# First expert's weights taken up later, an early partition maximum on GpSimd, and one more attention step ahead of the experts

## The chip, the cores and the metric

The kernel runs on 1 core of one Trainium2 chip. The metric is the device time of one execution in microseconds (us), and the time of a kernel is the median of several executions. The engines are named as in the profile: PE is TensorE, PEld its weight loads, DVE is VectorE, ACT is ScalarE, POOL is GpSimd, SP is SyncE, whose only work here is to issue DMAs.

## What is computed

Three layers follow each other. Attention in chunks of 64 tokens gives 4608 rows of 512; each row is sent to the best of 8 experts (two matrices with a ReLU between them, scaled by the gate); the result goes through an MLP with a piecewise quadratic activation.

```python
scores = scale * np.matmul(q_c, k_c.transpose(0, 1, 2, 4, 3))
attn = np.exp(scores - np.max(scores, axis=-1, keepdims=True))
attn = attn / (np.sum(attn, axis=-1, keepdims=True) + 1e-09)
x = np.matmul(attn, v_c)                      # then 4608 x 512
...
expert_idx = np.argmax(x @ w_gate, axis=1)    # 8 experts
for e in range(E):
    h = np.maximum(xe @ w1[e], 0.0)           # 512 -> 1024
    out[mask] = gate_w[mask, None] * (h @ w2[e])
...
h = x @ w_in                                  # 512 -> 2048
g = np.where(h >= 1, h, np.where(h <= -1, 0.0, (h + 1) ** 2 / 4))
return g @ w_out
```

## The kernel before

The order of the instructions on PE, ACT, DVE and SP is written out by the program itself (`manual_schedule`); each engine works through its own list from front to back, and an instruction that waits holds up all that stand behind it on its engine.

**Attention.** `attention_step(i)` works on one tile of 128 tokens, in stages of neighbouring tiles: the scores of tile i (L474), the transposed probabilities of tile i-1 (L482), the transposed result of tile i-3 (L502), the product with v of tile i-2 (L494), the gate logits of tile i-4 (L562) and the same by token for tile i-5 (L569). `vector_work(i)` adds what ACT does (copies `pt` L509, `xc` L513, the exponential `p` L522, `lt` L547) and what DVE does (row maximum `mx` L518, difference `p` L521, `rd` and `xr` L534 to L538). The 36 tiles are loaded in pairs: at each odd step SP issues q, k and v for a later pair, and it stores the finished pair `xr` to `xd` in DRAM (L541). The pool of `xr` has two buffers, so the buffer of one pair is written again three steps after its store was issued. Steps are numbered by the tile i in what follows.

**Gate.** The tiles are counted in batches of 6, 6, 6, 4, 6, 5 and 3. For each batch `gate(b)` works out on DVE the place of each token in the list of its expert (`m` to `slot`), with a few counting matmuls on PE in between (L594 to L598), and POOL scatters the tokens into `ld` in DRAM, one indirect DMA per tile (L635). After batch 0 the first expert is chosen; after batch 3 (`CUT_BATCH`) the rows of the first window of tokens are fetched: a list gather (L172), three row gathers `xg` (L149), a row maximum (`xam`, L102), the split into two half-precision parts (`xh`), and a DMA transpose into `xtw` (L168). After the last batch `rank_experts` orders the other experts and the second window is fetched in the same way.

**Experts' weights.** `fetch_experts` loads the eight pieces of the two matrices of an expert into seven buffers `raws` (L232, 512 KB each). `make_experts` turns them into two half-precision parts: four squares on ACT with a sum (L108, one per piece), the sum over pieces on DVE (`am_w`, L267), a maximum over the partitions on POOL (`partition_all_reduce`, L105, output `ag_w`), six small DVE operations that make a power of two of it (`kb` L79 to L90, `s_w`, `i_w` L91), then four times a high part on ACT (L111) and a low part on DVE (L114), which frees the buffer.

**What sets the order.** These background jobs are generators. A planner with four clocks (`clk`, in us of its own reckoning, PE's clock advanced by `slot`, 1.15 three times in an attention step) places each piece of background work when its engine's clock is not ahead of PE's by more than a slack, and not before the time that the job asks for. For a loaded piece of weights that time is the issue plus `WEIGHTS` (4.5). So a job's place in an engine's list is fixed when the program is built; on the chip its instruction waits if the data is late.

**Start of the experts.** The attention steps 0 to TAIL - 1 are written out ahead of the first window of the experts; from `HOLD` on, background jobs other than the urgent ones are held. `gate_tail` puts the remaining steps between the first matmuls of the first window, `ffn` L1000: each call of `beside` (after every three matmuls, or after the ReLU) advances it by one `yield`. The window is 384 tokens: 96 matmuls `h` (L1000), then 72 matmuls `y` (L1032). Then the second window of the same expert follows, then the other experts with their weights, and from about 620 us on the MLP (L1268, L1234).

Of the kernel before, what the change touches and what calls it, by code (L numbers as in the profile page):

```python
# [8 lines left out]
F32 = mybir.dt.float32  # L9
# [9 lines left out]
P = 128  # L19
NT = 36  # L20
# [18 lines left out]
AHEAD = 3  # L39
PACE = 3.5  # L40
LIST, ROWS, WEIGHTS = 2.2, 3.0, 4.5
LIST0, ROWS0 = 4.0, 9.0
SLACK = 0.3, 0.6
URGENT = 1.5
SIDE = 5, 7, 7
TAIL = NT + 2
HOLD = NT + 1
SIZES = {4: (4,), 5: (2, 3), 6: (3, 3), 7: (4, 3)}
ENOUGH = 11
# [7 lines left out]
def build(ctx, tc, qT, kT, v1, wg, w1, w2, wi, wo, out):  # L57
    nc = tc.nc
    pe, act, dve, pool, sp = nc.tensor, nc.scalar, nc.vector, nc.gpsimd, nc.sync
# [10 lines left out]
    with tc.manual_schedule(engines={E_.PE, E_.Activation, E_.DVE, E_.SP}):  # L70
# [33 lines left out]
        def allmax(dst, src):  # L104
            pool.partition_all_reduce(dst, src, channels=P, reduce_op=bass.bass_isa.ReduceOp.max)  # L105
# [11 lines left out]
        early = rows.enter_context(tc.tile_pool(name="early", bufs=1, side="right"))  # L117
# [10 lines left out]
        def raw_piece():  # L128
            nraw[0] += 1
            return raws_[:, (nraw[0] - 1) % NRAW]  # L130
# [98 lines left out]
        def load_weights(m, a, row):  # L229

            raw = raw_piece()
            sp.dma_start(out=raw, in_=(w1, w2)[m][a][bass.ds(row, P), :])  # L232
            return raw

        def first_row(idx):

            return nc.values_load(idx[0:1, 0:1], engines=[E_.SP], min_val=0, max_val=(E - 1) * P,
                                  skip_runtime_bounds_check_because="the place of one expert of E, times P")
# [41 lines left out]
        pieces, free = {}, [0.0] * NRAW  # L280

        def fetch_experts():

            for r in range(E):
                for m in range(2):
                    for a in range(4):
                        while not free or ready[0] < r:
                            yield 0.0, 0.0, 0.0, clk["pe"] + 0.5
                        yield 0.0, 0.0, 0.0, free.pop(0)
                        if m == 0 and a == 0:  # L290
                            row = first_row(widx[:, r:r + 1] if r else widx0)
                        pieces[r, m, a] = load_weights(m, a, row), clk["pe"] + WEIGHTS
                        if r == 0:
                            yield 0.0, 0.0, 0.0, clk["pe"] + PACE

# [22 lines left out]
        clk = {"pe": 0.0, "dve": 0.0, "act": 0.0, "pool": 0.0}  # L318
# [53 lines left out]
        with ExitStack() as ph:  # L372
# [60 lines left out]
            pid = const.tile([P, 1], F32, name="pid")  # L433
# [28 lines left out]
            pool.memset(pads[:, :, 1], 0)  # L462
            for t in xgs:
                pool.memset(t, 0.0)

            S, Pm, PT, O, X, XR, LG = {}, {}, {}, {}, {}, {}, {}
            xr = [None]
# [245 lines left out]
            def side(n):  # L713

                for g in list(sides):
                    while n:
                        try:
                            if next(g) == "wait":
                                break
                            n -= 1  # L720
                        except StopIteration:
                            sides.remove(g)
                            break

            def run_later():
                while later:
                    later.pop(0)()
# [28 lines left out]

            for i in range(TAIL):
                if i == HOLD:
# [3 lines left out]
        def gate_tail():  # L762

            for i in range(TAIL, NT + 6):
                attention_step(i)
                side(10 ** 9)
                for _ in range(3):
                    yield
            held.clear()
            while sides:  # L770
                run_later()
                now_step[0] += 1
                side(10 ** 9)
                yield
                yield
                yield
            rows.close()
            slack[0] = SLACK[1]
            background.insert(0, fetch(1))
            urgent.append(background[0])  # L780
# [3 lines left out]
        def overflow_plan():  # L784
# [15 lines left out]
            over["csum"], over["trips"] = csum, trips  # L800

        rest_of_gate = gate_tail()


# [65 lines left out]
        with ExitStack() as ph:  # L870
# [244 lines left out]
            r, k, size = windows[-1]  # L1115
# [57 lines left out]
        with ExitStack() as ph:  # L1173
# [85 lines left out]
            for g, nt in enumerate(GROUPS):  # L1259
# [3 lines left out]
                for f in range(16):  # L1263
# [6 lines left out]
                    r = rp.tile([P, 512], F32, name="r", tag="r")[:, 0:N]  # L1270
# [78 lines left out]
def emit(tc, a, out):  # L1349
    build(tc, a["qT"], a["kT"], a["v1"], a["wg"], [a[f"w1_{i}"] for i in range(4)], [a[f"w2_{i}"] for i in range(4)],  # L1350
          a["w_in"], a["w_out"], out)
# [26 lines left out]
```

## Time and profile before

| What | Value |
|---|---|
| Median of 3 runs | 1346.56 us |
| Lowest and highest of the 3 | 1346.37 and 1353.94 us |
| Profiled execution, own time | 1351.9 us |
| Its span, first to last instruction | 1350.2 us |
| Mean granted TensorE clock | 0.981 of full speed |
| Busy in the span | PE 1283.1, DVE 962.9, ACT 687.2, POOL 401.3 us |
| DMA | 148.20 MB, mean 110 GB/s |

The stretches used below are cut at 40, 77, 142, 157, 180, 227 and 620 us from the start of the span: plain attention; attention while the first expert's weights arrive; the fetch of the first window; the last full steps; the first window on PE; all later windows of the experts. A row of a timeline gives the start, the time to the end of a merged group, the engine, line and operation, and in brackets how long the engine had been idle before it and what ended the idleness.

### The profile page before, as it was taken

How to read it: one execution, taken by the hardware profiler on the slowest of the kernel's cores; microseconds unless marked ns; L12 is line 12 of the kernel's file. 1: busy time of each engine (PE TensorE's matmuls, PEld its weight loads, DVE VectorE, ACT ScalarE, POOL GpSimd, SP SyncE). 2: the span in 40 equal slices, each digit the busy share in tenths (PEclk: the TensorE clock that was granted, in tenths of full speed). 3: DMA queues.
4: the chain of work that ended last, by engine and by line, in shares of the span. 5: the costliest groups of instructions: out<-in, count | busy, mean ns of one | idle time of the engine just before them, and what ended most of it. 6: DMA issues, size and time to landing. Idle time of an engine off the chain costs nothing.

```text
span 1350.2 us, 23306 instructions
## 1 busy us (share of the span) xinstructions
PE 1283.1 (95%) x8839; PEld 800.3 (59%) x8839; DVE 962.9 (71%) x2127; ACT 687.2 (51%) x1325; POOL 401.3 (30%) x478
## 2 busy tenths in 40 slices
PE   6988887999999999998989999999999999999998
PEld 5767653445445446454464675848567584856757
DVE  5657763887787778775887767677676767767675
ACT  3446534765686666633464544545353454535344
POOL 3022233312223213111513506052341605234160
PEclk9989888999999999999989999999999999999999
DMA  9999637876676673213012030211103021110200
GB/s 210 295 277 305 173 90 227 249 231 221 173 239 214 174 234 104 55 55 96 1 28 67 1 94 1 56 40 36 60 7 88 1 60 36 40 55 9 55 1 32
DMA packets 127826, 148.20 MB, mean 110 GB/s; under 512 B 89164, under 2 KB 98380, under 8 KB 125664
## 3 DMA queue, kind: packets, MB, share of 16 engines
q1 hardware_dynamic: 119872, 127.40, 34.2%
q0 software_dynamic: 7840, 19.29, 4.4%
q8 instruction: 70, 1.15, 0.4%
q14 instruction: 44, 0.36, 0.1%
HBM read 99.10 MB, written 29.72 MB: 95 GB/s over the span
## 4 chain that ended last, share of the span: by engine, by line
PE 43%; DVE 5%; ACT 3%; POOL 2%; DMA 1%; issue 1%; ACTq 0%; POOLq 0%; DVEq 0%
PE h L1268 23%; PE o L1234 20%; POOL s L938 2%; DVE a L1277 1%; DVE r L1272 1%; ACT s L1197 1%; ACT r L1271 1%; DVE a L1198 1%; DVE raws L114 1%; DMA xtw<-xh 1%; DVE s L1198 1%; ACT a L1197 1%; ACT raws L111 0%; ACT xh L111 0%; DVE xh L114 0%
## 5 line engine op out<-in xcount | busy, mean ns | idle before, releaser
L1268 PE MATMUL h<-xtw,mlpw 128*128 128x512 f16 x1728 | 376.1, 380 | 3.5 <-ACT y L1020 3.5
L1268 PEld LDWEIGHTS <-mlpw 128*128 128x128 f16 x1728 | 169.5, 98 | 207.1 <-issue 6.1
L1000 PE MATMUL h<-xtw,wt 128*128 128x384 f16 (+2 forms) x1248 | 216.3, 335 | 16.8 <-DMA xtw<-xh 14.2
L1032 PE MATMUL y<-wt,ht 128*128 128x512 f16 x960 | 209.3, 379 | 0.0
L1271 ACT ACTIVATE r<-h,b_g,a_g 128x512 f32<-128x512 f32 x144 | 111.9, 777 | 169.2 <-PE h L1268 169.2
L1234 PEld LDWEIGHTS <-a 128*128 128x128 f16 x1728 | 166.5, 98 | 38.1 <-DVE a L1198 9.1
L1000 PEld LDWEIGHTS <-wt 128*128 128x128 f16 x1248 | 123.1, 99 | 107.9 <-issue 14.3
L938 POOL TENSOR_TENSOR s<-a,a 128x256 f32<-128x256 f32 x72 | 56.3, 782 | 433.5 <-PE h L1268 315.7
L1272 DVE SCALAR_TENSOR_TENSOR r<-r,kf_g 128x512 f32<-128x512 f32 x144 | 114.8, 797 | 80.7 <-ACT r L1271 80.7
L1032 PEld LDWEIGHTS <-ht 128*128 128x128 f16 x960 | 93.9, 98 | 112.1
L1197 ACT ACTIVATE s<-s 128x256 f16<-128x256 f32 x216 | 83.0, 412 | 128.8 <-POOL s L938 113.0
L1198 DVE TENSOR_TENSOR a<-a 128x256 f16<-128x256 f32 x288 | 116.3, 421 | 40.0 <-ACT a L1197 36.0
L1197 ACT ACTIVATE a<-a 128x256 f16<-128x256 f32 x288 | 112.8, 411 | 59.7 <-DVE a L1198 59.6
L1234 PEld LDWEIGHTS <-s 128*128 128x128 f16 x1296 | 127.6, 98 | 15.4
L1277 DVE SCALAR_TENSOR_TENSOR a<-h,c_g,r 128x256 f32<-128x256 f32 x288 | 126.2, 480 | 5.1
L1198 DVE TENSOR_TENSOR s<-s 128x256 f16<-128x256 f32 x216 | 94.4, 462 | 41.6 <-ACT s L1197 35.7
L1234 PE MATMUL o<-mlpw,a 128*128 128x256 f16 x864 | 99.8, 274 | 8.7 <-ACT a L1197 5.6
L1234 PE MATMUL o<-raws,a 128*128 128x256 f16 x864 | 99.2, 273 | 1.0 <-DVE a L1198 0.4
L1006 DVE SCALAR_TENSOR_TENSOR ht<-h,ht 128x384 f16<-128x384 f32 (+2 forms) x104 | 58.3, 562 | 57.9 <-ACT ht L1005 57.4
L1024 POOL DMA_INDIRECT yd<-y,list x40 | 42.2, 1054 | 186.0 <-ACT y L1020 157.2
L1234 PE MATMUL o<-mlpw,s 128*128 128x256 f16 x864 | 95.8, 273 | 0.0
L114 DVE SCALAR_TENSOR_TENSOR wt<-raws,s_w,wt 128x1024 f16<-128x1024 f32 x64 | 79.2, 1279 | 8.7 <-ACT wt L111 8.7
(177 smaller groups left out, 1518.2 us busy)
## 6 DMA issues: line engine op xcount, KB each, us to landing
raws<-w SPq DMA_DIRECT2D x64, 512.0 KB, 5.5
vbd<-v SPq DMA_DIRECT2D x36, 260.0 KB, 8.0
xd<-xr SPq DMA_DIRECT2D x18, 512.0 KB, 7.2
xg<-yd SPq DMA_DIRECT2D x36, 256.0 KB, 3.8
qt<-qT SPq DMA_DIRECT2D x16, 512.0 KB, 8.7
kbd<-kT SPq DMA_DIRECT2D x32, 256.0 KB, 8.8
mlpw<-w_out SPq DMA_DIRECT2D x8, 1024.0 KB, 5.9
mlpw<-w_in SPq DMA_DIRECT2D x8, 1024.0 KB, 4.8
```

The source lines that it names most:

```text
L114: dve.scalar_tensor_tensor(out=lo, in0=src, scalar=s, in1=hi, op0=ALU.mult, op1=ALU.subtract)
L938: pool.tensor_tensor(out=out, in0=a, in1=b, op=o)
L1000: pe.matmul(h[:, 0:N], lhsT=wa[:, a, wc:wc + P], rhs=xt[:, 4 * b + dc, 0:N], start=n == 0, stop=n == 11)
L1006: dve.scalar_tensor_tensor(out=lo, in0=h[:, 0:N], scalar=0.0, in1=hi, op0=ALU.max, op1=ALU.subtract)
L1032: pe.matmul(ys[t], lhsT=ht[:, a, f, c0 + t * P:c0 + (t + 1) * P], rhs=wb[:, b, f * D:(f + 1) * D], start=f == 0 and n == 0, stop=f == 7 an ...
L1197: act.activation(out=self.part(0, j, 0, n), in_=self.raw(j, n), func=AF.Copy)
L1198: dve.tensor_tensor(out=self.part(1, j, 0, n), in0=self.raw(j, n), in1=self.part(0, j, 0, n), op=ALU.subtract)
L1234: pe.matmul(y[:, i, :], lhsT=a.part(x, j, t * P, P), rhs=b.part(z, j), start=start and (j, i, n) == (0, 0, 0), stop=stop and (j, i, n) == ...
L1268: pe.matmul(h[:, 0:N], lhsT=w_in(a, dc, f), rhs=yt[:, 4 * b + dc, 0:N], start=n == 0, stop=n == 11)
L1271: act.activation(out=r, in_=h[:, 0:N], func=AF.Relu, scale=ci["a"], bias=ci["b"])
L1272: dve.scalar_tensor_tensor(out=r, in0=r, scalar=ci["sq"], in1=r, op0=ALU.min, op1=ALU.mult)
L1277: dve.scalar_tensor_tensor(out=x.raw(j, c.stop - c.start), in0=h[:, c], scalar=ci["c2"], in1=r[:, c], op0=ALU.mult, op1=ALU.max)
```

## The change

It has three parts. For the first expert (`r == 0`) a loaded piece is expected 14.0 instead of 4.5 after its issue, so its squares and all that hangs on them stand later in the lists. A partition maximum of the constant `pid` into a scratch tile `early_max`, which nothing reads, stands on POOL behind its constants at the start of the program. And TAIL grows by one: attention step 38 is written out ahead of the experts' first matmuls, and the steps 39 to 41 follow each other at two yields instead of three.

```diff
-LIST0, ROWS0 = 4.0, 9.0
+LIST0, ROWS0, WEIGHTS0 = 4.0, 9.0, 14.0
...
-TAIL = NT + 2
+TAIL = NT + 3
...
-                        pieces[r, m, a] = load_weights(m, a, row), clk["pe"] + WEIGHTS
+                        pieces[r, m, a] = load_weights(m, a, row), clk["pe"] + (WEIGHTS if r else WEIGHTS0)
...
             for t in xgs:
                 pool.memset(t, 0.0)
+            early_max = early.tile([P, 1], F32, name="early_max")
+            allmax(early_max, pid)
...
             for i in range(TAIL, NT + 6):
                 attention_step(i)
                 side(10 ** 9)
-                for _ in range(3):
+                for _ in range(2):
                     yield
```

Lines from 465 on stand two lower in the changed kernel, so L522 becomes L524 and L1000 becomes L1002. ACT's list from the exponential of step 16 on, before and then after; `raws` is a piece of the first expert's weights, and the row with `ss` is its square:

```order
L522 ACTIVATE p<-p 128x512
L108 ACTIVATE wt,ss<-raws 128x1024
L547 ACTIVATE lt<-la 128x128
L581 ACTIVATE L<-L 128x48
L509 ACTIVATE pt<-t 128x512
L513 ACTIVATE xc<-tx 128x512
L522 ACTIVATE p<-p 128x512
L547 ACTIVATE lt<-la 128x128
L108 ACTIVATE wt,ss<-raws 128x1024
```

The same place of the changed kernel, from the exponential of step 18 on:

```order
L524 ACTIVATE p<-p 128x512
L549 ACTIVATE lt<-la 128x128
L511 ACTIVATE pt<-t 128x512
L515 ACTIVATE xc<-tx 128x512
L524 ACTIVATE p<-p 128x512
L108 ACTIVATE wt,ss<-raws 128x1024
L549 ACTIVATE lt<-la 128x128
```

The first square moves from behind the exponential of step 16 to behind that of step 19; the fourth moves from step 20 to step 23.

POOL's list between the last memset of the start and the scatters of batch 4, before and then after; `ISA` without operands is the configuration of POOL that belongs to the partition maximum, `ag_w` the maximum for one of the first expert's two matrices:

```order
L464 MEMSET xg_94 128x512
L635 DMA ld<-tok,slot 40960x2 x12
L105 ISA
L105 ISA ag_w_1393<-am_w_1337 128x1
L635 DMA ld<-tok,slot 40960x2 x10
L172 DMA list<-ld,lidx_89 128x80
L105 ISA ag_w_1925<-am_w_1801 128x1
L149 DMA xg_90<-xd,list 128x512
L149 DMA xg_91<-xd,list 128x512
L149 DMA xg_92<-xd,list 128x512
```

The same place of POOL's list in the changed kernel:

```order
L464 MEMSET xg_94 128x512
L105 ISA
L105 ISA early_max<-pid 128x1
L637 DMA ld<-tok,slot 40960x2 x12
L105 ISA ag_w_1580<-am_w_1522 128x1
L637 DMA ld<-tok,slot 40960x2 x10
L172 DMA list<-ld,lidx_89 128x80
L149 DMA xg_90<-xd,list 128x512
L149 DMA xg_91<-xd,list 128x512
L149 DMA xg_92<-xd,list 128x512
L105 ISA ag_w_2079<-am_w_2029 128x1
```

The configuration now stands ahead of all scatters, and the second `ag_w` stands behind the three row gathers instead of ahead of them.

PE's list where the first window begins, before; `la` are the logits, `h` the experts' first product, `ones` and `zero` belong to the counting of batch 5:

```order
L569 MATMUL la<-sel_206,lt 128x8
L1000 LDWEIGHTS wt
L1000 MATMUL h_2418<-xtw,wt 128x384
L1000 LDWEIGHTS wt
L1000 MATMUL h_2418<-xtw,wt 128x384
L1000 LDWEIGHTS wt
L1000 MATMUL h_2418<-xtw,wt 128x384
L502 MATMUL tx<-ident,xr 128x128 x4
L562 MATMUL la<-xc,wgr 32x128 x4
L569 MATMUL la<-sel_206,lt 128x8
L594 LDWEIGHTS ones_171
L594 MATMUL la<-zero_173,ones_171 128x48
```

The same place of PE's list in the changed kernel:

```order
L571 MATMUL la<-sel_206,lt 128x8
L504 MATMUL tx<-ident,xr 128x128 x4
L564 MATMUL la<-xc,wgr 32x128 x4
L571 MATMUL la<-sel_206,lt 128x8
L596 LDWEIGHTS ones_171
L596 MATMUL la<-zero_173,ones_171 128x48
```

Step 38 and the counting of batch 5 now stand ahead of the first `h`. Further on, the counting of batch 6 stands behind 15 of the 96 matmuls `h` instead of behind 30.

Elsewhere the lists change as follows. On DVE the six operations from `kb` to `i_w` stand three steps later for each of the two matrices (for the second, at the end of step 32 instead of 29); the last two low parts of the first expert stand behind `rank_experts`, between the first `ht` of the first window. On SP the eighth piece of weights is issued one pair of tiles later.

## Rows read from the trace of the kernel before

**Rows 1.** Windows: us, busy us (count) of PE, PEld, DVE, ACT, POOL; PEclk, DMA share, GB/s.

```profile
40.00:77.00 37.00, 37.00 (x489) 29.35 (x487) 25.88 (x73) 18.40 (x39) 6.09 (x6) 0.96 1.04 294
77.00:142.00 65.00, 54.49 (x699) 43.63 (x693) 44.77 (x133) 36.92 (x77) 16.30 (x17) 0.92 0.98 290
142.00:157.00 15.00, 9.28 (x110) 7.58 (x108) 6.91 (x19) 7.15 (x13) 4.35 (x6) 0.77 0.54 149
157.00:180.00 23.00, 20.32 (x273) 15.76 (x267) 21.50 (x58) 12.37 (x25) 5.82 (x6) 1.00 0.51 118
180.00:227.00 47.00, 37.28 (x215) 19.53 (x215) 17.68 (x72) 13.77 (x27) 17.51 (x18) 0.89 0.54 156
227.00:620.00 393.00, 385.89 (x2030) 199.22 (x2029) 300.55 (x644) 252.88 (x411) 89.49 (x91) 0.99 0.59 177
```

**Rows 2.** Timeline of ACT, 76 to 106 us: the first and fourth square.

```profile
84.00 1.06 ACT L108 ACTIVATE wt<-raws 128x1024 bf16<-128x1024 f32 x1 [6.89 <-DMA raws<-w]
...
104.40 1.06 ACT L108 ACTIVATE wt<-raws 128x1024 bf16<-128x1024 f32 x1 [4.59 <-DMA raws<-w]
```

**Rows 3.** Timeline of PE, 73 to 157 us: scores of steps 16, 17, 31, 32, and waits.

```profile
73.72 1.09 PE L474 MATMUL s<-kbd,qt 128*64 128x128 f32 x16
...
77.48 1.09 PE L474 MATMUL s<-kbd,qt 128*64 128x128 f32 x16
...
86.05 0.66 PE L562 MATMUL la<-xc,wgr 128*32 128x128 f32 x8 [5.42 <-DVE eq L583]
...
145.52 1.09 PE L474 MATMUL s<-kbd,qt 128*64 128x128 f32 x16
152.34 1.12 PE L482 MATMUL t<-ident,p 128*128 128x128 f32 x4 [5.72 <-ACT p L522]
...
156.47 1.09 PE L474 MATMUL s<-kbd,qt 128*64 128x128 f32 x16
```

**Rows 4.** DMA issues, 60 to 150 us: count, KB each, median us to landing.

```profile
xd<-xr SPq DMA_DIRECT2D x10, 512.0 KB, 7.0
...
raws<-w SPq DMA_DIRECT2D x8, 512.0 KB, 8.6
```

**Rows 5.** Waits of DVE, 25 to 45 us: total us, times, longest.

```profile
DVE xr L538 <- DMA xd<-xr: 3.7, 1, 3.7
```

**Rows 6.** Timeline of POOL, 100 to 155 us: partition maxima, list and row gathers.

```profile
108.54 0.38 POOL L105 PARTITION_ALL_REDUCE ag_w<-am_w  x1 [6.82 <-issue]
...
147.34 0.98 POOL L172 DMA_INDIRECT list<-ld,lidx  x1 [5.34 <-DMA xd<-xr]
148.37 0.30 POOL L105 PARTITION_ALL_REDUCE ag_w<-am_w  x1
150.51 1.05 POOL L149 DMA_INDIRECT xg<-xd,list  x1 [1.83 <-issue]
...
153.18 0.99 POOL L149 DMA_INDIRECT xg<-xd,list  x1 [0.30 <-issue]
```

**Rows 7.** Timeline of DVE at 148 us: the second matrix's power of two.

```profile
148.71 0.15 DVE L79 TENSOR_SCALAR kb<-ag_w 128x1 int32<-128x1 int32 x1 [6.38 <-POOL ag_w L105]
```

**Rows 8.** Timeline of PE, 182 to 227 us: first window, then second.

```profile
182.74 1.12 PE L1000 MATMUL h<-xtw,wt 128*128 128x384 f16 x3 [2.68 <-DMA xtw<-xh]
...
193.03 10.88 PE L1000 MATMUL h<-xtw,wt 128*128 128x384 f16 x66
203.75 15.70 PE L1032 MATMUL y<-wt,ht 128*128 128x512 f16 x72
226.50 17.70 PE L1000 MATMUL h<-xtw,wt 128*128 128x384 f16 x96 [7.04 <-DMA xtw<-xh]
```

**Rows 9.** Timeline of POOL, 188 to 205 us: scatters of batches 5 and 6, list gather.

```profile
188.31 0.96 POOL L635 DMA_INDIRECT ld<-tok,slot  x1 [12.78 <-DVE slot L633]
...
195.37 0.96 POOL L635 DMA_INDIRECT ld<-tok,slot  x1 [1.07 <-DVE c L668]
...
204.34 0.98 POOL L172 DMA_INDIRECT list<-ld,lidx  x1 [5.48 <-DMA ld<-tok,slot]
```

## The prediction

> **What bounds the kernel now.** I read the windows by stage first, to see where PE is not busy. From 227 to 620 us PE is busy for 385.89 of 393 us, so there the kernel is bound by PE and whatever is gained earlier should arrive at the end almost whole. The stretches ahead of it are different: PE is busy 54.49 of 65 us from 77 to 142, 9.28 of 15 from 142 to 157, and 37.28 of 47 from 180 to 227 [rows 1]. The reader is to see there three holes, and the timelines name what ends each.
>
> First hole: ACT stands still for 6.89 and for 4.59 us in front of two squares of the first expert's weights, whose DMAs have not landed [rows 2]. ACT's list is worked in order, so the copies that PE needs stand behind the square, and PE waits 5.42 us [rows 3]. One attention step takes 77.48 - 73.72 = 3.76 us when nothing is late. The 14 steps from the scores of step 17 at 77.48 to those of step 31 at 145.52 take 68.0 us; 14 x 3.76 is 52.6, and three groups of counting matmuls come to some 0.9 (an estimate), so 14.5 us are lost, 11.5 of them by the two waits of ACT.
>
> Second hole: step 31 takes 156.47 - 145.52 = 10.95 us instead of 3.76, so 7.2 are lost; PE waits 5.72 of them for the exponential [rows 3]. Behind that is a chain through POOL: the list gather stands waiting for DMAs until 147.34, the partition maximum `ag_w` of the second matrix stands behind it at 148.37 [rows 6], DVE has waited 6.38 us for that at `kb` [rows 7], and the exponentials stand behind DVE and ACT.
>
> Third hole: PE waits 2.68 us before the first expert window and 7.04 before the second, both times for the DMA transpose `xtw` [rows 8]. The second wait hangs on the end of the gate: the scatters of batch 6 start at 195.37, the list gather can go at 204.34 [rows 9], the rows reach PE at 226.50.
>
> **The change, part by part.** *Squares later.* The same eight loads and squares remain; the squares stand three steps later, by 3 x 3.76 = 11.3 us more than before. The first loads were issued some 8.6 us ahead of their landing [rows 4], and waits of 6.9 and 4.6 us are both shorter than 11.3, so both ACT waits should be gone, unless loads become slower by over 4 us. What is late next is the DMA itself. From 40 to 77 us the 16 DMA engines show a busy share of 1.04, which I take for "never without work", and 0.98 from 77 to 142 [rows 1]. So in these 65 us they were without work for only 65 x 0.06 / 1.04 = 3.75 us, and the same bytes must be moved in any case. That is the low end of the gain: 3.75. Beyond it the steps may run ahead only as far as the queue may grow. The tightest user is the store of `xr`: its buffer is written again three steps later, about 11.3 - 0.7 = 10.6 us after the issue, and the store takes 7.0 us in the median [rows 4]; DVE did wait 3.7 us for it where the queue was longer, at 25 to 45 us [rows 5]. That leaves 2 to 3 us of growth. I take 3.75 + 2.25 = 6. The high end is the whole 11.5 of the two waits, if the share overstates how full the engines are. The Trainium skill (DMA: Bandwidth & Descriptors, Where 436 GB/s comes from) puts the limit of moves between HBM and SBUF at about 358 GB/s for a core; the 290 GB/s of this stretch stand well below that, so by the page the DMA would have room and this term would be 11.5 and not 6. I go by the share in the rows, and keep the page's reading as a rival.
>
> *The second `ag_w`.* `kb` of the second matrix moves three steps later on DVE, from about 142.3 (148.71 - 6.38) to 142.3 + 11.3 = 153.6 in the old times. On POOL `ag_w` now stands behind the three row gathers, whose last one ends at 153.18 + 0.99 = 154.2 [rows 6], so it is there at about 154.8: a wait of 1.2 us in place of 6.38, and some more if the list gather lands later, because the loads that the old stall let drain are then still in the queue. I charge 2, so 7.2 - 2 = 5.2 remain as gain. Bounds: 7.2 (no wait left) and 2.2 (the gathers 5 us late, as the list gather itself was).
>
> *The early maximum.* It adds one POOL instruction of 0.3 to 0.4 us and moves POOL's configuration, behind which the first `ag_w` shows 6.82 us of "issue" [rows 6], to the start, where POOL has nothing until the scatters of batch 0. I give it no term of its own: the 6.82 us are over 2.8 us after the `am_w` that they hold up, and that loss is inside the first hole, which the DMA caps. If this cover were not there it would be worth those 2.8 us. POOL's start holds no one up: its memsets come first, and PE waits there for loads.
>
> *Step 38 ahead, and the gate's end.* No work is added: step 38 and the counting of batch 5 (1.4 and 0.5 us of PE) move into the hole in front of the first `h`, which waits for `xtw` at 182.74 anyway [rows 8]. Batch 5's places no longer wait for those first matmuls, so its five scatters, 1.26 us each with the gaps, start some 4 us earlier than 188.31, about 184.2, and end about 190.5. The counting of batch 6 stands behind 15 `h` instead of 30, so its places are known some 6 us earlier, about 189.3, but POOL is free only at 190.7. So the scatters of batch 6 start 195.37 - 190.7 = 4.7 us earlier, and the chain behind them to 226.50 is unchanged. I take 4.5. PE is not later than that: 96 `h` at 10.88 / 66 = 0.165 us are 15.9, the last `y` starts by about 201 even if PE waits 2 us for an `ht` behind the two low parts that now stand there, and 15.70 us of `y` [rows 8] end at about 217, before the second window at 222. Bounds: 2.5 (DVE's two low parts, 1.27 us each, fall on the chain) and 6 (POOL no longer decides).
>
> *Later.* From 227 us on all is the same work in nearly the same order; 7 of 393 us are idle, and I charge nothing.
>
> The sum is 6 + 5.2 + 4.5 = 15.7 us. Against the profiled execution's 1351.9 us (span 1350.2 and 1.7 around it) that gives 1336.2. This execution is 5.3 us above the median of the runs, 1346.56, and I put the forecast on the median: 1346.56 - 15.7 = 1330.9, say 1331. The low bounds add to 3.75 + 2.2 + 2.5 = 8.5 (1338), the high ones to 11.5 + 7.2 + 6 = 24.7 (1322).
>
> **Rivals.** *The DMA has room.* The whole 11.5 us of the ACT waits go: 11.5 + 5.2 + 4.5 = 21.2, so 1325. For it: single stretches move more than the mean of 290 GB/s, and attention from 40 to 77 us kept PE fully busy. Against it: the share of 0.98, and the store that DVE had to wait for. Chance 0.20.
>
> *The stalls come back as others.* DMA gives 3.75 only, the three gathers ahead of `ag_w` are late, and the low parts fall on the gate's end: 8.5 us, so 1338. For it: everything in these 150 us shares one DMA queue and one POOL. Chance 0.23.
>
> *The early maximum does not keep what it fetches.* If POOL has to be configured again at the first `ag_w`, 6.8 us stand between `am_w` and `kb`, which are now only some 1.3 us of DVE work apart: about 5.9 us back on DVE, 15.7 - 5.9 = 9.8, so 1337. Against it: the configuration stands once in POOL's list, and later maxima after indirect DMAs show no such gap (0.30 us at 148.37). Chance 0.05.
>
> *Slower: the stores of `xr` decide.* If the squares no longer hold the attention back, the queue may grow until each pair of tiles waits for its buffer, as DVE did for 3.7 us [rows 5]. This decides from a time to landing of 10.6 us on; at 14.3 us it costs 3.7 us a pair, 26 us for the seven pairs from step 17 to 30, against 14.5 lost there now. With the other two terms the total is 26 - 14.5 - 9.7, so 1.8 slower, 1348; with a lower clock after each wait it could be 20 us. Against it: the bytes are the same, so such waits can't last longer than the DMA needs, which is less than the time it takes now. Chance 0.07.
>
> **How the numbers follow.** My forecast has the remaining 0.45. About 1%, 13.5 us, is what a measurement of this kernel tells from no change. Of the forecast's own cases (12 to 19 us) some seven in ten are beyond that, with the first rival 0.52 in all, and I add a little for gains that the lower clock after each wait gives back (PEclk is 0.77 from 142 to 157 and 0.89 from 180 to 227 [rows 1]): 0.55 faster, 0.41 within 1%, 0.04 slower. The range is 1322 to 1341: the high bounds below, the second and third rival and 3 us for the spread of runs above.
>
> **What would show it.** Right: ACT shows no wait of over 1 us for `raws` before 130 us; the DMA share from 77 us on is 1.0 or more until the last loads; steps 17 to 31 take about 62 us; `kb` of the second matrix waits 1 to 3 us; POOL's configuration stands near 13 us; the second window starts about 15 us earlier than 226.50, and from there to the end the time is as before. Wrong: steps 17 to 31 in about 56 us (the DMA had room), waits of DVE at `xr` for `xd` of several us (the stores decide), a `kb` that waits over 4 us, or a gain at 227 us that is gone at 620.

## The result, and the profile after

The changed kernel takes 1337.96 us (median of 7 runs, 1331.7 to 1342.89) against 1346.56 us before (7 runs, 1342.9 to 1353.94). The ratio is 0.9918, 95% interval 0.9896 to 0.994, so the change is worth 8 to 14 us, and 8.6 by the medians: under 1%, and 7 us above the forecast of 1331, though inside its range (1322 to 1341). It stands where the rival "The stalls come back as others" had put it (1338). On two other chips, further down, the same pair of kernels gave 0.9941 and 0.9942.

The profiled execution of the changed kernel took 1342.89 us, the slowest of its 7 runs; its span is 1341.2 us. The stages, cut where the prediction cut them (us, from the timelines of PE):

| Stage | before | after | difference |
|---|---|---|---|
| start to the scores of step 17 | 77.48 | 72.66 | -4.82 |
| scores of step 17 to scores of step 31 | 68.04 | 69.48 | +1.44 |
| scores of step 31 to scores of step 35 | 22.65 | 23.33 | +0.68 |
| scores of step 35 to first `h` | 14.57 | 14.52 | -0.05 |
| first `h` to second window | 43.76 | 39.11 | -4.65 |
| second window to the end | 1123.7 | 1122.1 | -1.6 |

The two spans differ by 9.0 us, which looks like the measured gain. But over half of it, 4.82, lies ahead of the first instruction that the change moves on PE, ACT and DVE. Four other profiles used below reach step 17 at 73.0 to 75.03 us, two of them of kernels without the early maximum (74.18 and 75.03), so the profile of before had a slow start. The three profiles with the maximum do start sooner (72.66 to 73.81), but the kernel with the maximum alone is at most 1.9 us faster than before, by its 95% interval further down. So no more than 1.9 of the 4.82 us can be the change's. What is left is the gate's end; the steps from 17 to 35, where the prediction saw 11.2 us, show no gain in this pair. The scores of step 35 before, from PE's timeline:

```profile
168.17 1.09 PE L474 MATMUL s<-kbd,qt 128*64 128x128 f32 x16
```

Windows by stage of the changed kernel (busy us and count of PE, PEld, DVE, ACT, POOL; PEclk, DMA share, GB/s), to be held against [rows 1]:

```profile
77.00:142.00 65.00, 55.73 (x672) 44.17 (x668) 42.35 (x123) 35.50 (x71) 16.94 (x17) 0.89 1.02 279
142.00:157.00 15.00, 10.81 (x142) 8.74 (x142) 6.57 (x18) 5.85 (x13) 4.31 (x5) 0.99 0.71 206
...
180.00:227.00 47.00, 42.05 (x219) 21.88 (x220) 23.56 (x72) 16.85 (x29) 18.86 (x19) 0.89 0.61 204
227.00:620.00 393.00, 384.07 (x2021) 197.83 (x2020) 298.45 (x652) 250.65 (x406) 86.55 (x92) 0.99 0.59 172
```

From 77 to 142 us PE is hardly busier than before (55.73 against 54.49), at a lower granted clock (0.89 against 0.92), and the DMA shows no idle time: its share went from 0.98 to 1.02.

ACT's squares, which waited 6.89 and 4.59 us [rows 2], now find their data there; no row of this stretch has a bracket for `raws`:

```profile
85.64 1.04 ACT L108 ACTIVATE wt<-raws 128x1024 bf16<-128x1024 f32 x1
...
89.28 1.05 ACT L108 ACTIVATE wt<-raws 128x1024 bf16<-128x1024 f32 x1
```

DVE waits instead. Its timeline, 76 to 160 us; `xr` waits for the store of the pair before the last, `kb` for the partition maximum [rows 5, 7]:

```profile
82.12 0.69 DVE L540 TENSOR_TENSOR xr<-ob,rd 128x512 f32<-128x512 f32 x1 [1.77 <-DMA xd<-xr]
...
92.28 0.69 DVE L540 TENSOR_TENSOR xr<-ob,rd 128x512 f32<-128x512 f32 x1 [3.44 <-DMA xd<-xr]
...
103.18 0.69 DVE L540 TENSOR_TENSOR xr<-ob,rd 128x512 f32<-128x512 f32 x1 [4.18 <-DMA xd<-xr]
...
124.55 0.69 DVE L540 TENSOR_TENSOR xr<-ob,rd 128x512 f32<-128x512 f32 x1 [3.56 <-DMA xd<-xr]
...
155.57 0.15 DVE L79 TENSOR_SCALAR kb<-ag_w 128x1 int32<-128x1 int32 x1 [5.34 <-POOL ag_w L105]
```

The four waits at `xr` add to 12.95 us, more than the 11.48 of ACT that went. DMA issues of the changed kernel, 60 to 150 us (count, KB each, median us to landing): a store of `xr` now takes 10.2 us instead of 7.0, a piece of weights 11.1 instead of 8.6 [rows 4]. The trace tells the landing of only four of these ten stores and two of these eight pieces; in the kernel with the weights alone, further down, it tells nine stores, and their median is 10.1.

```profile
xd<-xr SPq DMA_DIRECT2D x10, 512.0 KB, 10.2
...
raws<-w SPq DMA_DIRECT2D x8, 512.0 KB, 11.1
```

PE's timeline of the changed kernel: the scores of steps 17, 31 and 35, the long waits between them, and the first expert windows [rows 3, 8]:

```profile
72.66 1.09 PE L476 MATMUL s<-kbd,qt 128*64 128x128 f32 x16
...
104.02 0.63 PE L504 MATMUL tx<-ident,xr 128*128 128x128 f32 x4 [3.19 <-DVE m L577]
...
142.14 1.09 PE L476 MATMUL s<-kbd,qt 128*64 128x128 f32 x16
...
158.57 0.65 PE L564 MATMUL la<-xc,wgr 128*32 128x128 f32 x8 [5.76 <-DVE eq L585]
...
165.47 1.09 PE L476 MATMUL s<-kbd,qt 128*64 128x128 f32 x16
...
179.99 0.70 PE L1002 MATMUL h<-xtw,wt 128*128 128x384 f16 x3 [0.51 <-DMA xtw<-xh]
...
199.23 15.70 PE L1034 MATMUL y<-wt,ht 128*128 128x512 f16 x72
...
219.10 3.38 PE L1002 MATMUL h<-xtw,wt 128*128 128x384 f16 x10 [4.16 <-DMA xtw<-xh]
```

The wait of 5.72 for the exponential [rows 3] is now one of 5.76 for the gate, both behind `kb`. The waits between steps 17 and 31 have a second price, the granted clock of TensorE. Windows in which it stood at 0.50, the lower of its two levels (1.2 of 2.4 GHz), before:

```profile
83.70:90.50 6.80, 4.45 (x44) 3.75 (x45) 4.82 (x19) 4.36 (x10) 0.00 (x0) 0.50 0.99 276
107.60:110.90 3.30, 3.30 (x24) 2.97 (x23) 1.78 (x8) 1.01 (x1) 0.38 (x1) 0.50 1.03 252
```

The same of the changed kernel; they begin soon after PE waited 3.19 us, until 104.02, and 2.87 us, until 125.39:

```profile
105.40:112.10 6.70, 6.70 (x63) 5.30 (x61) 4.22 (x14) 3.51 (x8) 0.35 (x1) 0.50 1.04 277
125.90:132.60 6.70, 6.70 (x60) 5.54 (x59) 6.23 (x23) 2.20 (x6) 0.00 (x0) 0.50 1.02 286
```

Between steps 17 and 31 PE waited 10.4 us before and 9.3 after. It worked at the lower level for 7.75 us before and 13.40 after, where the 16 matmuls of a step's scores take 1.98 us instead of 1.09. If all this work would have taken half as long at the upper level, the clock cost 3.9 and 6.7 us (an estimate). Waits and clock add to 14.3 and 16.0 us, close to what these steps lost by the prediction's count, 14.5 and 15.9. So PE did wait 1.1 us less, and the clock took more than that back.

The wait before the first `h` fell from 2.68 to 0.51, since step 38 stands in it, and that before the second window from 7.04 to 4.16 [rows 8].

POOL's timeline of the changed kernel [rows 6, 9]:

```profile
20.50 0.38 POOL L105 PARTITION_ALL_REDUCE early_max<-pid  x1 [7.58 <-issue]
...
110.90 0.35 POOL L105 PARTITION_ALL_REDUCE ag_w<-am_w  x1 [19.62 <-DVE am_w L267]
...
145.52 0.98 POOL L172 DMA_INDIRECT list<-ld,lidx  x1 [7.04 <-DMA vbd<-v]
151.57 1.02 POOL L149 DMA_INDIRECT xg<-xd,list  x1 [5.07 <-DMA vbd<-v]
...
154.20 1.00 POOL L149 DMA_INDIRECT xg<-xd,list  x1 [0.30 <-issue]
155.23 0.31 POOL L105 PARTITION_ALL_REDUCE ag_w<-am_w  x1
...
187.96 0.95 POOL L637 DMA_INDIRECT ld<-tok,slot  x1 [0.30 <-DVE c L670]
...
196.59 0.98 POOL L172 DMA_INDIRECT list<-ld,lidx  x1 [4.84 <-DMA ld<-tok,slot]
```

The configuration lies from 12.9 to 20.5 us, and the first `ag_w` waits only for its data. The list gather waits 7.04 us (5.34 before), the first row gather another 5.07 (1.83 before), by the profile both for loads of v, and the second `ag_w` behind them is late for `kb`. The scatters of batch 6 stand right behind those of batch 5.

### The profile page after: what moved, and what is told of

Read it like the earlier page. It is cut to its first block, busy times and chain, and to the rows that moved or that the text cites. A ratio compares the mean times of both kernels' runs of the same rounds, so it can differ in the third digit from the quotient of the medians.

```text
span 1341.2 us, 23314 instructions
## 1 busy us (share of the span) xinstructions
PE 1283.2 (96%) x8839; PEld 800.6 (60%) x8839; DVE 963.2 (72%) x2127; ACT 689.9 (51%) x1325; POOL 399.7 (30%) x479
## 3 DMA queue, kind: packets, MB, share of 16 engines
q8 instruction: 70, 1.15, 0.4%
## 4 chain that ended last, share of the span: by engine, by line
PE 43%; DVE 5%; ACT 3%; POOL 2%; DMA 1%; issue 1%; ACTq 0%; POOLq 0%; DVEq 0%
PE h L1270 23%; PE o L1236 20%; POOL s L940 2%; DVE a L1279 1%; DVE r L1274 1%; ACT s L1199 1%; ACT r L1273 1%; DVE a L1200 1%; DVE raws L114 1%; DMA xtw<-xh 1%; DVE s L1200 1%; ACT a L1199 1%; ACT raws L111 0%; ACT xh L111 0%; DVE xh L114 0%
## 5 line engine op out<-in xcount | busy, mean ns | idle before, releaser
L1002 PE MATMUL h<-xtw,wt 128*128 128x384 f16 (+2 forms) x1248 | 214.5, 334 | 10.4 <-DMA xtw<-xh 8.8
L1002 PEld LDWEIGHTS <-wt 128*128 128x128 f16 x1248 | 123.0, 99 | 100.6 <-issue 10.1
```

Source lines behind the costliest of these rows:

```text
L1002: pe.matmul(h[:, 0:N], lhsT=wa[:, a, wc:wc + P], rhs=xt[:, 4 * b + dc, 0:N], start=n == 0, stop=n == 11)
```

## The experiments

The theory after this profile (A): the DMA is full from 40 us to the end of the loads, so a wait taken from ACT comes back at `xr` and at POOL's gathers, and only the gate's end is a gain. Its rivals: the weights' delay alone is worth 6 to 11 us and something else gave it back (B); the early maximum speeds up the start (C).

### One part at a time

Four kernels on one chip, where before took 1349.56 us (median of 35 runs). The weights alone:

```diff
-LIST0, ROWS0 = 4.0, 9.0
+LIST0, ROWS0, WEIGHTS0 = 4.0, 9.0, 14.0
...
-                        pieces[r, m, a] = load_weights(m, a, row), clk["pe"] + WEIGHTS
+                        pieces[r, m, a] = load_weights(m, a, row), clk["pe"] + (WEIGHTS if r else WEIGHTS0)
```

> The kernel before with WEIGHTS0 = 14 alone. Theory A (the DMA bounds the steps while the first expert's weights arrive, so the waits only move from the squares to the stores of xr, and the second stall only moves behind the gathers): the squares no longer wait for raws, DVE waits 10 us or more in sum at xr for xd, steps 17 to 31 take 66 to 71 us as before, and the median is within 3 us of the kernel before. Rival B (this part is worth its forecast, and the one profile was an unlucky execution): steps 17 to 31 in about 62 us, the time 6 to 11 us shorter than before.

Measured: 1346.64 us, ratio 0.9973 (0.9949 to 0.9997), so 3.6 us (0.4 to 6.9) less. Waits of its DVE, 72 to 175 us (total, times, longest):

```profile
DVE xr L538 <- DMA xd<-xr: 9.9, 3, 4.1
...
DVE kb L79 <- POOL ag_w L105: 2.9, 1, 2.9
```

Its PE timeline, the scores of steps 17, 31 and 35:

```profile
75.03 1.09 PE L474 MATMUL s<-kbd,qt 128*64 128x128 f32 x16
...
139.49 1.09 PE L474 MATMUL s<-kbd,qt 128*64 128x128 f32 x16
...
160.70 1.09 PE L474 MATMUL s<-kbd,qt 128*64 128x128 f32 x16
```

Steps 17 to 31 take 64.46 us and 31 to 35 21.21: 3.58 and 1.44 less than before, and not 6 and 5.2. The two terms that hang on the weights were forecast at 11.2 us together; the interval excludes that. Between A and B this run is less clear: the squares no longer wait and DVE waits 9.9 us at `xr`, as A had it, but the steps are shorter than A's 66 to 71 us, the time is at the edge of A's 3 us, and its interval reaches into B's 6 to 11.

Up to step 38 the lists of PE, ACT and DVE are the same here as in the changed kernel, which took 5.0 us longer for steps 17 to 31. PE waited 8.8 us in them here and 9.3 there, so the waits don't make this difference. The granted clock does: here it stood at 0.50 in one short window.

```profile
124.90:128.20 3.30, 3.30 (x40) 2.53 (x36) 3.09 (x12) 2.00 (x5) 0.00 (x0) 0.50 1.04 331
```

By the estimate above that costs 1.7 us, against 6.7 in the changed kernel. So a single profile does not size this term. The four profiles without the weights' part, with the same lists up to there, scatter as well: 66.45 to 70.31 us. The sizes have to come from the medians.

The early maximum alone:

```diff
+            early_max = early.tile([P, 1], F32, name="early_max")
+            allmax(early_max, pid)
```

> The kernel before with the early partition maximum alone. Theory A: POOL's configuration moves to about 13 us, the first ag_w follows its am_w at once, which removes a wait of some 2 to 3 us inside a DMA-bound stretch: 0 to 2 us shorter. Rival C (the shorter start of the profile after, 4.8 us to step 17, comes from this part): 4 to 5 us shorter, and step 17 near 72.7 us in its profile.

Measured: 1349.69 us, ratio 1.001 (0.9986 to 1.0033), so between 1.9 us less and 4.5 more. C falls by the time: it wanted 4 to 5 us less. Its profile alone would not have told, since it reaches step 17 at 73.0 us, near C's 72.7. The part moves the configuration, and that is worth nothing that can be told. POOL's first `ag_w`, in this kernel:

```profile
101.67 0.35 POOL L105 PARTITION_ALL_REDUCE ag_w<-am_w  x1 [4.45 <-DVE rd L536]
```

What is named there is the last update of DVE's semaphore; `ag_w` reads `am_w`.

In the kernel with the weights alone the same row stands at 108.22 with 16.32 us of waiting for DVE and none of "issue": once the squares are late, the row shows nothing of the configuration, which stands where it stood before; it fits into POOL's idle time.

The tail alone:

```diff
-TAIL = NT + 2
+TAIL = NT + 3
...
-                for _ in range(3):
+                for _ in range(2):
```

> The kernel before with TAIL = NT + 3 and two yields alone. Theory A: from the first h of the first window to the first h of the second 39 us instead of 43.8, and the time 4 to 5.5 us shorter. Rival B (half of the gain comes from the weights): 4 to 5.5 us as well; this run sizes the third term by itself. If the low parts behind rank_experts made the difference, it is under 3.

Measured: 1344.52 us, ratio 0.9956 (0.9936 to 0.9977), so 5.9 us (3.1 to 8.6) less. ACT's waits for `raws` are all there (13.2 us in two), and the windows of the first expert stand 38.45 us apart, as in the changed kernel:

```profile
184.53 0.65 PE L1000 MATMUL h<-xtw,wt 128*128 128x384 f16 x3 [0.50 <-DMA xtw<-xh]
...
222.98 7.20 PE L1000 MATMUL h<-xtw,wt 128*128 128x384 f16 x31 [5.82 <-DMA xtw<-xh]
```

The changed kernel without the weights' part:

```diff
-                        pieces[r, m, a] = load_weights(m, a, row), clk["pe"] + (WEIGHTS if r else WEIGHTS0)
+                        pieces[r, m, a] = load_weights(m, a, row), clk["pe"] + WEIGHTS
```

> The changed kernel without its WEIGHTS0, that is the early maximum and the tail. Theory A: as fast as the changed kernel within 3 us (5 to 9 us shorter than before). Rival B: slower than the changed kernel by 6 us or more, that is within 4 us of the kernel before.

Measured: 1343.46 us, ratio 0.9951 (0.9928 to 0.9974), so 6.6 us less; 39.21 us between the windows, and ACT waits 10.3 us for `raws` again. The three parts alone add to 3.6 - 1.3 + 5.9 = 8.2 us, near what the whole gives on three chips (7.9 to 11.0 by the ratios). They add up, and by the point values the tail carries the greater part; the intervals of the weights (0.4 to 6.9) and the tail (3.1 to 8.6) overlap.

### Fewer bytes, and more room for the stores

Whether the DMA's rate holds steps 17 to 31 was to be shown by taking the bytes away, beside the changed kernel itself and one with more buffers for `xr`. These ran on another chip, where before took 1356.74 us (18 runs). Fewer bytes:

```diff
-        def load_weights(m, a, row):
+        def load_weights(m, a, row, n=1024):
...
-            sp.dma_start(out=raw, in_=(w1, w2)[m][a][bass.ds(row, P), :])
+            sp.dma_start(out=raw[:, 0:n], in_=(w1, w2)[m][a][bass.ds(row, P), 0:n])
...
-                        pieces[r, m, a] = load_weights(m, a, row), clk["pe"] + (WEIGHTS if r else WEIGHTS0)
+                        pieces[r, m, a] = load_weights(m, a, row, 1024 if r else 64), clk["pe"] + (WEIGHTS if r else WEIGHTS0)
...
+            for k in range(NRAW):
+                pool.memset(raws_[:, k], 1.0)
```

> The changed kernel, with 64 instead of 1024 columns of each row of the first expert's weights loaded (a sixteenth of the bytes; the rest of the buffers holds ones, so the first expert's products are left out in effect). All instructions on PE, ACT, DVE and POOL stay as they are. Theory A (the DMA bounds steps 17 to 31: the stall moved from ACT to the stores of xr): no wait of DVE at xr over 1 us between 77 and 142 us, steps 17 to 31 in 54 to 58 us instead of 69.5, a DMA share of 0.8 or less there, the list gather not waiting for loads and kb of the second matrix waiting under 2 us instead of 5.3; the whole 12 to 18 us below the changed kernel's profile. Rival D (the steps are bound by the engines' lists, by the work of the weights on ACT and DVE or by the granted clock): steps 17 to 31 stay at 64 us or more with so few bytes.

> The changed kernel once more, unchanged, to set it beside the next two on one chip and to see what a second profile of it shows. Theory A: median 1338 to 1342, ratio about 0.994; second window 39 us behind the first again, steps 17 to 35 in 88 to 93 us, DVE waiting at xr for 5 us or more in sum. If the parts add (weights -3, maximum 0, tail -5) the ratio is 0.994; the 0.992 first measured lies within its interval.

Measured: with a sixteenth of the bytes 1350.05 us (one run), steps 17 to 31 in 66.24 us, no wait at `xr` over 1 us from 77 us on; the changed kernel 1346.35 us, ratio 0.9941 (0.9914 to 0.9969), steps 17 to 31 in 67.13 us, and no such wait at `xr` either. With few bytes the steps are as long as D had them, but not for the reasons that D names, and that the changed kernel itself shows no wait at `xr` is what neither theory had. In both profiles PE has gaps of its own; the section on the hardware shows such rows. So this pair could not tell, and it was run again on a third chip, where before took 1356.97 us (15 runs):

> The changed kernel with a sixteenth of the first expert's weights loaded, once more: in its first profile PE had gaps with nothing released by another engine (6.5 us between 40 and 142 us), which no earlier profile of another kernel showed, so it could not tell. Theory A (DMA): where PE shows no such gaps, steps 17 to 31 in 54 to 60 us and no wait at xr; timed, 5 to 12 us below the changed kernel on the same chip. Theory E (the supply of PE's instructions, or the lists, bound these steps): 64 us or more again, and timed within 3 us of the changed kernel.

> The changed kernel unchanged, as the reference of this call. Ratio 0.991 to 0.995. Theory A: where PE shows no gaps without a releaser, DVE waits at xr for 5 us or more in sum between 77 and 142 us; where it shows them, the DMA gains on PE meanwhile and the waits at xr are gone.

Measured: 1346.67 us with few bytes (ratio 0.9911, 0.9878 to 0.9945; steps 17 to 31 in 67.62 us), 1348.17 us for the changed kernel (0.9942, 0.9919 to 0.9964; 66.55 us). The windows 77 to 142 us of the two, few bytes first:

```profile
77.00:142.00 65.00, 59.16 (x717) 45.94 (x715) 44.70 (x131) 35.82 (x71) 15.99 (x16) 0.92 0.81 227
```

```profile
77.00:142.00 65.00, 59.80 (x711) 46.21 (x711) 45.74 (x133) 36.45 (x73) 16.95 (x17) 0.92 0.97 283
```

The DMA share fell from 0.97 to 0.81, PE's work in the stretch did not change, and the time is 1.5 us lower with intervals that overlap: what theory E expected. So on this chip the bytes of the weights do not hold the steps. What does is in part PE's own gaps: 4.9 us of them in the changed kernel from 77 to 142 us, and in the same stretch a granted clock of 0.92. The steps lost 13.0 us by the prediction's count (66.55 against 53.5), so a part stays open. That the gaps give the transfers time, and so end the waits at `xr`, fits but is not shown. On the chip of the first comparison, where PE has no such gaps, that the DMA holds them is read from the rows (share 1.02, landing at 10.2 us, 12.95 us of waits at `xr`), and no run here shows it by an experiment.

Three buffers for `xr`:

```diff
-        xrp = rows.enter_context(tc.tile_pool(name="xrp", bufs=2, side="right"))
+        xrp = rows.enter_context(tc.tile_pool(name="xrp", bufs=3, side="right"))
```

> The changed kernel with three buffers for xr instead of two, so a pair may wait two steps longer for its store. If only the two buffers hold the steps (the queue could grow without harm): no wait at xr, steps 17 to 31 in 56 to 60 us, the time 8 to 12 us below the changed kernel's. Theory A (the DMA's rate holds them): the waits at xr go, but others take their place (PE or DVE for q, k, v, or ACT for raws, or the list gather for longer), steps 17 to 35 in 86 to 92 us, the time within 3 us of the changed kernel's.

Measured: 1343.48 us, ratio 0.9899 (0.9864 to 0.9933), 2.9 us below the changed kernel on the same chip, with intervals that overlap. Steps 17 to 35 take 89.29 us against 86.63. Since the changed kernel has no wait at `xr` on this chip either, this says nothing about the chip of the first comparison, where it has.

### The power of two one step later

```diff
-URGENT = 1.5
+URGENT, LATE = 1.5, 4.0
...
-            yield 0.9, 0.0, 0.0, clk["pool"] + 0.3
+            yield 0.9, 0.0, 0.0, clk["pool"] + (LATE if name == "w1" and not ranked else 0.3)
```

It was run with the third buffer on the second chip, and alone and with it on the third:

> The same with three buffers for xr, and the six operations from kb on of the first expert's second matrix asked for 4.0 instead of 0.3 us behind POOL's maximum in the planner's reckoning: one attention step later on DVE. If the wait at kb is a real loss: it is under 1.5 us instead of 5.3, steps 31 to 35 take 18 to 20 us instead of 23.3, and the time is 3 to 4 us below the same kernel without this. If the gathers on POOL set the start of the experts in any case: the wait goes, but the first matmul of the experts then waits for xtw by as much as is gained, and the time is the same within 1.5 us.

> The changed kernel with the six operations from kb on of the first expert's second matrix one attention step later, and nothing else. If the wait at kb is a real loss of 5.3 us: steps 31 to 35 take 18 to 20 us, kb waits under 2.5 us, and the time is 2 to 5 us below the changed kernel's. If the row gathers set the start of the experts: steps 31 to 35 are shorter by as much as the stretch from step 35 to the first expert matmul is longer, and the time is the same within 1.5 us.

> The later kb and three buffers for xr together, once more beside the kernel with the later kb alone. If the third buffer is worth what the first call let it seem (1343.5 against 1346.4): another 2 to 4 us below the kernel with the later kb alone. If it only moves the waits: the same within 1.5 us. Against before a ratio of 0.985 to 0.989.

Measured: 1338.93 us (ratio 0.9867, 0.9824 to 0.9909) with the third buffer on the second chip; on the third chip 1340.73 us alone (0.9887, 0.986 to 0.9914) and 1340.31 us with it (0.9873, 0.9851 to 0.9895). Alone it is 7.4 us below the changed kernel of the same set (1348.17), and the two intervals do not touch, if only just: this kernel beats both. On the second chip it is 4.6 us below the kernel with the third buffer alone, with intervals that overlap. The third buffer adds nothing to it that can be told. Where the gain lies stays open. In the profiles steps 31 to 35 take 16.59 us against 20.74, shorter still than the 18 to 20 expected, but the stretch from step 35 to the first `h` takes 19.96 against 16.58, as the other theory had it. `kb` waits in neither; with the third buffer on the second chip it waits 2.41 us. The scores of step 35 and the first `h`, first of the changed kernel and then of the kernel with the later `kb`:

```profile
164.52 1.98 PE L476 MATMUL s<-kbd,qt 128*64 128x128 f32 x16
...
181.10 0.65 PE L1002 MATMUL h<-xtw,wt 128*128 128x384 f16 x3 [0.42 <-DMA xtw<-xh]
```

```profile
162.45 1.09 PE L476 MATMUL s<-kbd,qt 128*64 128x128 f32 x16
...
182.41 1.12 PE L1002 MATMUL h<-xtw,wt 128*128 128x384 f16 x3
```

These profiles are of executions that lie 9.6 us below and 3.3 us above the medians of their kernels (1338.57 us for the changed kernel with its median of 1348.17, and 1344.04 with 1340.73). The profiled execution of the faster kernel is thus the slower of the two, and they can't show the gain.

## Why the prediction was off

**What held.** The diagnosis of the three holes and each order of instructions came as told: no wait of ACT for `raws`, a DMA share of 1.02, the configuration from 12.9 us on, the second `ag_w` behind the row gathers, nothing lost between 227 and 620 us. The third term is right: 4.5 us were forecast for step 38 and the gate's end, the stretch between the two windows is 4.65 us shorter, and the tail alone measures 5.9 (3.1 to 8.6). That the early maximum has no term of its own is borne out as well, within 1.9 us less to 4.5 more. The rival about a configuration that does not last falls: the later maxima take 0.31 to 0.35 us each and show no such gap.

**Term 1, the squares (6 us forecast).** The step that failed is "Beyond it the steps may run ahead only as far as the queue may grow ... That leaves 2 to 3 us of growth", which was booked as gain on top of 3.75. The prediction itself had the point from which a pair waits, 10.6 us to landing; the median of the stores went to 10.2. From there on what ACT no longer waits is waited for at `xr`: 11.48 us went, 12.95 came, and steps 17 to 31 took 69.48 us where about 62 were forecast. The term also has no entry for the granted clock, which the prediction names only in a rival and for its chances. It puts 11.5 of the 14.5 us lost before down to ACT's two waits; PE's own waits behind them were 5.42 and 2.41 us, and most of the rest was the clock. In the changed kernel the clock cost 6.7 us of these steps, by the estimate above, and 1.7 with the weights alone, where they took 64.46. Its size is told by the medians alone: with the weights alone terms 1 and 2 are worth 3.6 us (0.4 to 6.9) together, where 11.2 were forecast; how the 3.6 divide between them is not shown. The share of 1.02 at 279 GB/s also speaks against the rival in which the DMA has room. By the rate of the Trainium skill (DMA: Bandwidth & Descriptors, Where 436 GB/s comes from), about 358 GB/s, there would have been room; the share in this trace, 1.02 at 279 GB/s, does not agree. That the DMA is what holds these steps is read from such rows and not shown by an experiment.

**Term 2, the second `ag_w` (5.2 us forecast).** The step that failed is the time of the last row gather, carried over from before. There it ended 154.17 - 145.52 = 8.65 us behind the scores of step 31; in the changed kernel it ended 155.20 - 142.14 = 13.06 us behind them, since the list gather and the first row gather waited longer, by the profile for loads of v that were still under way. These 4.4 us on top of the forecast wait of 1.2 make 5.6, and `kb` waited 5.34. The prediction had charged 0.8 us for exactly this ("some more if the list gather lands later") and had 5 as its bound; the value came near the bound. In the two later profiles of the changed kernel the last gather ends 8.06 and 7.92 us behind step 31 and `kb` does not wait, so the size of this term changes from profile to profile. In those two the DMA share from 77 to 142 us was 0.98 and 0.97 instead of 1.02, which would fit a queue that was less full.

**The rivals.** Time and mechanism are those of "The stalls come back as others", with one difference: the low parts did not fall on the gate's end. That the time fits so well is partly luck: the rival's 8.5 us are 5.95 from the weights and 2.5 from the gate's end, and the parts alone measured 3.6 and 5.9. The mechanism of the slower rival, pairs that wait for their buffer, is what happened to term 1, at 1.77 to 4.18 us a wait; the steps came out at 69.48 us, near the 68.0 of before, as the argument against that rival had it.

**What the table of stages would have taught wrongly.** Without the kernels with one part each, the 4.82 us at the start might have been counted as the change's, and the forecast would have seemed wrong in place rather than in two sizes.

## What to carry to other kernels

Where one stall hangs on a transfer and the profile shows the engines of the DMA as already full (here a share of 0.98), moving the work that waits can move the wait: book only the DMA's idle time as gain, and look for the next user of the queue (here a store with two buffers, and the gathers behind it). A stall that moves also moves the places where the granted clock falls, so count that beside the wait. Two waits that were taken to hang on the same queue gave 3.6 us where 11.2 were booked, while a gain that hangs on another resource, here POOL's free time at the gate's end, came whole. And a difference between two profiles counts only from the first instruction that the change moves.

## What was not expected of the hardware

PE had gaps that nothing in the kernel explains, and only on two of the chips. Those two chips ran one set of kernels each, so chip and set can't be told apart. PE's timeline of the changed kernel on the third chip, behind the scores of step 20; `issue` is time in which PE waited for nothing that the profile shows:

```profile
88.84 1.09 PE L476 MATMUL s<-kbd,qt 128*64 128x128 f32 x16
...
90.89 0.64 PE L496 MATMUL ob<-vbd,pt 128*64 128x130 f32 x5
92.57 0.45 PE L496 MATMUL ob<-vbd,pt 128*64 128x130 f32 x3 [1.04 <-issue]
94.00 0.46 PE L496 MATMUL ob<-vbd,pt 128*64 128x130 f32 x4 [0.97 <-issue]
94.72 0.27 PE L496 MATMUL ob<-vbd,pt 128*64 128x130 f32 x1 [0.27 <-issue]
95.43 0.45 PE L496 MATMUL ob<-vbd,pt 128*64 128x130 f32 x3 [0.44 <-issue]
...
96.48 1.85 PE L476 MATMUL s<-kbd,qt 128*64 128x128 f32 x16
```

The 16 matmuls `ob` come in small groups some 0.7 or 1.4 us apart instead of within 1.1 us, and the scores behind them take 1.85 us instead of 1.09, with the granted clock at 0.50 from 96.70 to 100.00 us. DVE stands idle here too: a row maximum starts at 95.53 after 5.47 us of idle time, ended by an update that the profile gives to no instruction. Such gaps lie behind the scores of steps 15, 20 and 27 in all eight profiles of the second and third chip, whatever the kernel: 3.1 to 6.0 us of such gaps from 77 to 142 us. The six profiles of the first comparison and the first set, kernels with and without the change among them, show 0.0. Before took 7 to 10 us longer on those two chips, which fits the gaps, though no profile of before was taken there.

It looks like a late supply of instructions, but that is not shown. The Trainium skill (Runtime: NRT & Kernel Launch, Instruction fetch mechanics) says that an engine's instructions are fetched in blocks of 16 KiB over its own DMA queue, at a cost that is mostly hidden. The trace agrees on the blocks: the page of the changed kernel has 70 packets and 1.15 MB in one instruction queue, 16.4 KB each; it does not tell whose instructions they are.

```profile
q8 instruction: 70, 1.15, 0.4%
```

The count is the same in the profiles with gaps and without, so what makes the gaps on two chips stays open.
